# Dealing out the first loads anew, and idle matmuls that read a constant, in a local attention and gated feed-forward kernel

## The chip, the cores and the metric

The kernel runs on one core of a Trainium2 chip. The metric is device time in microseconds (us), from launch to end; three runs of the kernel before gave 213.14, 213.52 and 213.74 us.

The core has five engines that run beside each other and wait for each other through semaphores: TensorE (PE in the profile) for matrix products, VectorE (DVE), ScalarE (ACT), GpSimd (POOL) and SyncE (SP), which here issues transfers and otherwise computes nothing. Transfers (DMA) are issued by SyncE, ScalarE and GpSimd, each of which has a queue of its own.

## The reference

The input `x` has 2048 rows of 512 numbers. It is normalised by rows, and the result feeds two branches. One is an attention of 32 heads of 16 numbers in which each row sees itself and seven earlier rows, two apart. The other is a gated feed-forward layer. The two are multiplied and added to the input. Cut to what matters:

```python
xn = _layernorm(x, axis=-1)
qkv = xn @ wqkv                       # 512 -> 3 * 512, split into q, k, v of 32 heads
logits = einsum("bhsd,bhswd->bhsw", q, kg) * scale   # kg: k at s, s-2, ..., s-14
attn = softmax(where(mask, logits, -1e9))
s = einsum("bhsw,bhswd->bhsd", attn, vg) @ wo
h = gelu(xn @ w_gate) * (xn @ w_up)   # 512 -> 1792
g = silu(h @ w_down)                  # 1792 -> 512
return x + s * g
```

All inputs and the output are bf16.

## The kernel before

The 2048 rows are cut into four blocks `j` of 512 (`TQ`), and each block into four tiles of 128 rows. A block goes through these stages: normalise and transpose (`layernorm`, for tiles 0 and 1 `early_tile`), q, k and v (`qkv`, for block 0 tile by tile in `qkv_tiles`), the scores and their softmax (`scores`), the weighted sum over v (`values`), the feed-forward layer (`ffn` and `down`), and the product of the two branches with the addition of `x` and the store (`out`).

No stage is issued when it is written. Each piece of work is declared as an `Op` with a name, an engine, an estimated duration, the names that it needs (with a `~` in front: only the start of that piece), and a priority. The function `schedule` then deals these out in order of estimated time, with the priorities as tie-breakers, and the instructions are emitted in that order; so each engine has one fixed order. The figures of `PARAMS` (base priorities by stage and block, and one `nudge` for each `Op`) set the priorities.

The names that matter for this change:

- `warm` (L246) declares five pieces, `warm0` to `warm4`, of idle matmuls: their product is never read. They keep TensorE working until the first transposes. Four pieces have two matmuls of 128 x 512 columns each, the last has one of 256. Their operand is `blank`, a tile that VectorE fills with zeros (L1222) at the start of the program, ahead of the fill of `eps` (L1223).
- `preset` (L262) is an activation on ScalarE without a use of its own; it makes the table for the square root load early. In the plan it stands behind the start of `ld_wqa`.
- `early_tile` (L423) handles tiles 0 and 1 in halves of 256 columns: statistics, root, scaling, two transposes for each half (`turn`), and the copy into `xT0` (`copy`).
- `qkv_tiles` (L572) multiplies each tile by wq, wk and wv, 16 matmuls of 128 columns for each (L584). For q and k of tile 0, and q of tile 1, it is cut into two pieces of eight, such as `mm_k0_t0a` and `mm_k0_t0`: the first needs the first half of the weight (`ld_wka`) and of the transposed tile, the second needs the rest.
- `loads` (L1106) issues all loads of the inputs, in the order of the list `seq`. `ld_x0_0a` and `ld_x0_0b` are the two halves of tile 0 of `x`, `ld_wqa` and `ld_wq` the two halves (256 KB each) of wq, and so on. Before the change SyncE issues both halves of tile 1, wk, the tiles 2 and 3 as one load of 256 KB, wv and all that follows; ScalarE issues the second half of tile 0 and both halves of wq.
- `out` (L1009) ends in a store of each block: two stores of 256 KB for blocks 0 to 2, smaller ones for block 3.

In the lists below, a "full" matmul moves 512 columns, a small one 128.

Of the kernel before, what the change touches and what calls it, by code (L numbers as in the profile page):

```python
# [13 lines left out]
BF16 = mybir.dt.bfloat16  # L14
F32 = mybir.dt.float32

P = 128
# [4 lines left out]
TQ = 512  # L22
# [8 lines left out]
NC = D // P  # L31
NF = DF // P
NJ = S // TQ
TPB = TQ // P
# [26 lines left out]
    sums=(3,), psum=(0,), warm=4, slack=3.5, N=[267.5, 33.2, 480.8, 875.4], S=[194.3, -690.4, 43.8, -317.7],  # L61
    V=[-45.5, -104.1, 270.7, -195.0], Q=[-3.6, -356.0, 73.8, 32.5], F=[86.8, 80.1, 275.5, 543.3],
    Y=[-111.3, 10.6, -115.3, -110.9], O=[33.1, -472.0, -324.1, 458.9], vnorm=(), vcopy=(2,), vsum=(0,),
    crowd=1.35,
    nudge=[
# [162 lines left out]
class Kernel:  # L228
# [17 lines left out]
    def warm(self):  # L246


        def mms(i):
            if i == 0:  # L250
                self.new("warm", [P, TQ], F32, "warm_ps")
            n = TQ // 2 if i == self.par["warm"] else TQ
            for _ in range(1 if i == self.par["warm"] else 2):
                self.nc.tensor.matmul(
                    self.t["warm"][:, 0:n], lhsT=self.blank[:, 0:P], rhs=self.blank[:, 0:n], start=True, stop=True
                )

        for i in range(self.par["warm"] + 1):
            self.op(f"warm{i}", "PE", 0.95 if i < self.par["warm"] else 0.2, [f"warm{i - 1}"] if i else [], lambda i=i: mms(i),
                    take=[("F", "warm")] if i == 0 else [], use=["warm"], prio=1e6)  # L260

    def preset(self):  # L262

        self.op("preset", "ACT", 0.2, ["warm0", "~ld_wqa"], lambda: self.nc.scalar.activation(
            out=self.spare[:], in_=self.eps[:], func=AF.Sqrt), prio=-1e6, table="sqrt")
# [16 lines left out]
    def layernorm(self, j):  # L282
        base = self.when("N", j)
        for tt in range(TPB):
# [90 lines left out]
            else:  # L375
                self.op(f"stats{t}", "DVE", 0.61,
                        [f"ld_x{j if j else 2}_{j}"] + {2: ["copy1"], 3: ["~aggr2"]}.get(t, ["~rstd3"]), stats, prio=prio,
# [631 lines left out]
    def out(self, j):  # L1009
# [32 lines left out]
        if j < NJ - 1:  # L1042
# [9 lines left out]

            def store(i, j=j):
                a = j * TQ + i * 2 * P
                self.nc.sync.dma_start(
                    out=self.out2d[a : a + 2 * P, :].rearrange("(t p) d -> p t d", p=P),
                    in_=self.t[f"s16{j}"][:, 2 * i : 2 * i + 2, :],
                )
# [5 lines left out]
            for i in range(2):  # L1064
                self.op(f"store{j}_{i}", "SP", 0.35, [f"add{j}"], lambda i=i, f=store: f(i), use=[f"s16{j}"],
                        nbytes=P * TPB * D, kind="out")
# [39 lines left out]
    def loads(self, src):  # L1106
# [28 lines left out]
        def w_o():  # L1135
# [4 lines left out]
        early = [(f"ld_x{t}_0{'ab'[i]}",  # L1140
                  lambda t=t, i=i: x_tile(t, i * D // 2, (i + 1) * D // 2, "sync" if t or not i else "scalar"),
                  64 * kb if t else kb) for t in range(2) for i in range(2)]
        h = NC // 2
        wq = [("ld_wqa", lambda: w_qkv(0, 0, h, "scalar"), 256 * kb), ("ld_wq", lambda: w_qkv(0, h, NC, "scalar"), 256 * kb)]
        wk = [("ld_wka", lambda: w_qkv(1, 0, h), 256 * kb), ("ld_wk", lambda: w_qkv(1, h, NC), 256 * kb)]
# [128 lines left out]
```

## Time and profile before

| what | value |
|---|---|
| median of three runs | 213.52 us |
| lowest, highest | 213.14, 213.74 us |
| the profiled execution | 213.6 us |
| its span, first to last instruction | 211.8 us |
| TensorE busy | 206.1 us (97%) |
| VectorE busy | 187.6 us (89%) |
| ScalarE busy | 150.3 us (71%) |
| GpSimd busy | 65.5 us (31%) |
| read from memory, written | 14.12 MB, 6.31 MB |

The profile comes from one execution of its own. Its span runs from the first instruction to the last; the time of a run is longer by what lies around the span, here 1.8 us. Matmuls overlap each other, so that a duration of a single one is longer than the distance to the next: what counts for the time is the distance. Rows of the timeline merge neighbouring instructions of the same kind, and give the start, the length of the whole group, and the count. A transfer has two rows: its issue on a queue (SPq, ACTq, POOLq) and its landing, given as the time from issue to landing.

### The profile page before, as it was taken

To read this page: it belongs to the slowest core of one execution; us is meant where nothing else is said; L and a number is where in the kernel's file an instruction comes from. 1 tells how busy PE (TensorE), PEld (TensorE's weight loads), DVE (VectorE), ACT (ScalarE), POOL (GpSimd) and SP (SyncE) were. 2 spreads that over 40 slices of the span, in tenths; PEclk is the share of its full clock that TensorE was granted. 3 is DMA by queue.
4 is the path that set the end of the run, shared out by engine and by line. 5 is a ranking of instruction groups with operands and counts; after the bars stand their busy time and mean duration, and the time that the engine had idled before them with its cause. 6 is when DMAs were issued, how large, how long until landed. Compare 5 with 4: busy or idle time off the path is not lost.

```text
span 211.8 us, 3074 instructions
## 1 busy us (share of the span) xinstructions
PE 206.1 (97%) x1105; PEld 102.0 (48%) x1123; DVE 187.6 (89%) x218; ACT 150.3 (71%) x257; POOL 65.5 (31%) x107
## 2 busy tenths in 40 slices
PE   7999999999999999999999999999999999999994
PEld 2896443445444444444444444444444444444442
DVE  4788998869999998999999999999999999997024
ACT  3587957999999899766905489966614489859051
POOL 5034200002115787440459520479730011001000
PEclk9999999999999999999999999999999999999999
DMA  5999999203802888962898865358797069708903
GB/s 182 348 382 373 298 280 240 50 3 74 173 25 73 186 135 144 178 192 38 144 114 135 166 173 115 99 99 162 143 192 163 0 104 231 163 0 149 249 4 99
DMA packets 33119, 32.17 MB, mean 152 GB/s; under 512 B 17088, under 2 KB 29648, under 8 KB 33104
## 3 DMA queue, kind: packets, MB, share of 16 engines
q0 software_dynamic: 5136, 14.41, 35.8%
q1 hardware_dynamic: 27136, 16.95, 31.0%
q10 hardware_dynamic: 832, 0.62, 1.0%
q8 instruction: 9, 0.15, 0.3%
q14 instruction: 6, 0.05, 0.1%
HBM read 14.12 MB, written 6.31 MB: 96 GB/s over the span
## 4 chain that ended last, share of the span: by engine, by line
PE 94%; DMA 2%; SPq 1%; issue 1%; DVE 0%; ACT 0%
PE g_ps L900 23%; PE y_ps L960 23%; PE u_ps L900 23%; PE qkv_ps L500 15%; PE s_ps L1021 6%; PE qkv_ps L584 5%; DMA wk_sb<-in_A_wqkv_dram 2%; SPq L1110 1%; PE L_ps L716 0%; PE tr_ps L345 0%; SPq L1120 0%; DVE s L1076 0%; ACT sil L976 0%; DVE s L1082 0%
## 5 line engine op out<-in xcount | busy, mean ns | idle before, releaser
L900 PE MATMUL g_ps<-xnT,wg_sb 128*128 128x512 bf16 x221 | 54.2, 379 | 0.2
L900 PE MATMUL u_ps<-xnT,wu_sb 128*128 128x512 bf16 x217 | 52.7, 379 | 0.3
L960 PE MATMUL y_ps<-wd_sb,hT 128*128 128x512 bf16 (+2 forms) x233 | 51.4, 366 | 0.2
L916 ACT ACTIVATE gl<-g_ps 128x512 bf16<-128x512 f32 x56 | 32.6, 598 | 18.6 <-PE g_ps L900 10.8
L772 POOL DMA_DIRECT2D Ls<-prod x48 | 36.3, 844 | 29.0 <-DMA Ls<-prod 9.8
L677 DVE TENSOR_TENSOR prod<-q_sb,k_sb 128x2048 bf16<-128x2048 bf16 x32 | 38.0, 1216 | 0.7 <-ACT q_sb L515 0.7
L924 ACT ACTIVATE hT<-u_ps 128x512 bf16<-128x512 f32 x56 | 32.4, 601 | 7.2 <-PE u_ps L900 6.6
L843 DVE TENSOR_TENSOR pv<-attn,v_arr 128x4096 bf16<-128x4096 bf16 x16 | 36.1, 2283 | 0.0
L960 PEld LDWEIGHTS <-hT 128*128 128x128 bf16 x238 | 22.8, 98 | 25.9
L900 PEld LDWEIGHTS <-wu_sb 128*128 128x128 bf16 x224 | 21.8, 98 | 26.6 <-issue 0.4
L900 PEld LDWEIGHTS <-wg_sb 128*128 128x128 bf16 x224 | 21.9, 98 | 26.2
L938 DVE TENSOR_TENSOR hT<-hT,gl 128x1024 bf16<-128x1024 bf16 x28 | 18.8, 683 | 1.3 <-ACT gl L916 1.1
L691 DVE TENSOR_TENSOR prod<-prod 128x2048 bf16<-128x2048 bf16 x16 | 19.2, 1214 | 0.0
L1021 PE MATMUL s_ps<-wo_sb,oT_sb 128*128 128x512 bf16 (+2 forms) x68 | 15.1, 366 | 0.1
L976 ACT ACTIVATE sil<-y_ps 128x512 bf16<-128x512 f32 (+2 forms) x17 | 9.1, 576 | 8.6 <-PE y_ps L960 8.5
L850 DVE TENSOR_TENSOR pv<-pv 128x2048 bf16<-128x2048 bf16 x12 | 14.3, 1215 | 0.0
L649 POOL DMA_DIRECT2D v_arr<-vT_dram x16 | 10.9, 700 | 10.4 <-DMA vT_dram<-vst 10.0
L866 POOL DMA_DIRECT2D pv<-pv x4 | 3.6, 894 | 30.6 <-DVE pv L843 30.1
L515 ACT ACTIVATE q_sb<-qkv_ps 128x512 bf16<-128x512 f32 x12 | 7.1, 624 | 8.2 <-PE qkv_ps L500 8.2
L1036 ACT ACTIVATE s<-s_ps 128x512 bf16<-128x512 f32 x15 | 8.9, 602 | 5.4 <-PE s_ps L1021 5.4
L500 PE MATMUL qkv_ps<-xnT,wv_sb 128*128 128x512 bf16 x48 | 12.3, 379 | 0.0
L542 POOL DMA_DIRECT2D vT_dram<-vst x12 | 7.2, 605 | 15.7 <-ACT vst L522 15.7
(91 smaller groups left out, 231.9 us busy)
## 6 DMA issues: line engine op xcount, KB each, us to landing
Ls<-prod POOLq DMA_DIRECT2D x48, 128.0 KB, 3.7
v_arr<-vT_dram POOLq DMA_DIRECT2D x16, 142.0 KB, 4.2
vT_dram<-vst POOLq DMA_DIRECT2D x16, 128.0 KB, 3.6
pv<-pv POOLq DMA_DIRECT2D x4, 512.0 KB, 5.4
oT_dram<-o_sb SPq DMA_DIRECT2D x16, 128.0 KB, 3.4
oT_sb<-oT_dram SPq DMA_DIRECT2D x4, 512.0 KB, 4.8
wg_sb<-in_B_w_gate_dram SPq DMA_DIRECT2D x2, 896.0 KB, 10.6
wu_sb<-in_B_w_up_dram SPq DMA_DIRECT2D x2, 896.0 KB, 12.5
```

Source lines behind the costliest of these rows:

```text
L500: self.nc.tensor.matmul(ps[:], lhsT=self.w_qkv(which, dk, c), rhs=self.t[f"xT{j}"][:, dk, :], start=(dk == 0), stop=(dk == NC - 1),)
L677: self.nc.vector.tensor_tensor(out=self.t[pair][:, c % 2].rearrange("p n w t -> p w n t"), in0=q.unsqueeze(1).to_broadcast([P, W, 2, P]), ...
L691: self.nc.vector.tensor_tensor(out=pr[:, 0], in0=pr[:, 0], in1=pr[:, 1], op=ALU.add)
L772: self.nc.gpsimd.dma_start(out=self.t[f"Ls{j}"][H * tq : H * (tq + 1)], in_=self.t[f"pr{j}_{tq // 2}_0"][s::NC, 0, tq % 2], **(dict(accum_ ...
L843: self.nc.vector.tensor_tensor(out=pv[:], in0=self.t[f"at{j}"][:, 2 * i : 2 * i + 2, :].unsqueeze(2).to_broadcast([P, 2, DH, P]), in1=win, ...
L850: self.nc.vector.tensor_tensor(out=pv[:, 0], in0=pv[:, 0], in1=pv[:, 1], op=ALU.add)
L900: nc.tensor.matmul(ps[:], lhsT=w[:, dk, fc * P : (fc + 1) * P], rhs=self.t[f"xT{j}"][:, dk, :], start=(dk == 0), stop=(dk == NC - 1),)
L916: self.nc.scalar.activation(out=self.t[f"gl{j}_{pair}"][:, fc % 2, :], in_=self.t[f"ps_g{j}_{fc}"][:], func=AF.Gelu_apprx_tanh,)
L924: self.nc.scalar.activation(out=self.t[f"h{j}"][:, fc, :], in_=self.t[f"ps_u{j}_{fc}"][:], func=AF.Copy)
L938: self.nc.vector.tensor_tensor(out=h, in0=h, in1=self.t[f"gl{j}_{pair}"][:], op=ALU.mult)
L960: nc.tensor.matmul(self.t["ps_" + key][:, 0 : n1 - n0], lhsT=self.t[f"h{j}"][:, fc, tt * P : (tt + 1) * P], rhs=self.wd_sb[:, fc, n0:n1], ...
L1021: self.nc.tensor.matmul(ps[:, 0 : n1 - n0], lhsT=self.t[f"oT{j}"][:, c, tt * P : (tt + 1) * P], rhs=self.wo_sb[:, c, n0:n1], start=(c == 0 ...
```

## The change

Five things change.

1. The idle matmuls read a constant one that the program's own prologue writes into a single column, seen as a tile of 128 x 512 by strides of zero. `blank` and its fill are gone. `warm0` has three matmuls instead of two.
2. `preset` is planned behind the start of `ld_x1_0b`.
3. The first loads are dealt to the two queues in turn: SyncE has `x0` first half, `x1` first half, wq second half, wk second half; ScalarE has `x0` second half, wq first half, `x1` second half, wk first half. Tiles 2 and 3 of `x` become two loads of 128 KB on SyncE, and the statistics of each need only its own.
4. The store of block 0 is one of 512 KB instead of two of 256 KB.
5. All figures of the plan in `PARAMS` are new, among them all 858 nudges.

```diff
 PARAMS = dict(
-    sums=(3,), psum=(0,), warm=4, slack=3.5, N=[267.5, 33.2, 480.8, 875.4], S=[194.3, -690.4, 43.8, -317.7],
+    sums=(3,), psum=(0,), warm=4, slack=3.42, N=[236.5, 17.4, 498.7, 880.9], S=[216.5, -699.2, 31.7, -311.4],
...
             n = TQ // 2 if i == self.par["warm"] else TQ
-            for _ in range(1 if i == self.par["warm"] else 2):
+            ones = self.nc.const_aps.tensor(1.0, [P, TQ], BF16)
+            for _ in range(1 if i == self.par["warm"] else 2 if i else 3):
                 self.nc.tensor.matmul(
-                    self.t["warm"][:, 0:n], lhsT=self.blank[:, 0:P], rhs=self.blank[:, 0:n], start=True, stop=True
+                    self.t["warm"][:, 0:n], lhsT=ones[:, 0:P], rhs=ones[:, 0:n], start=True, stop=True
                 )
...
-            self.op(f"warm{i}", "PE", 0.95 if i < self.par["warm"] else 0.2, [f"warm{i - 1}"] if i else [], lambda i=i: mms(i),
+            self.op(f"warm{i}", "PE", 1.28 if i == 0 else 0.85 if i < self.par["warm"] else 0.2, [f"warm{i - 1}"] if i else [], lambda i=i: mms(i),
...
-        self.op("preset", "ACT", 0.2, ["warm0", "~ld_wqa"], lambda: self.nc.scalar.activation(
+        self.op("preset", "ACT", 0.2, ["~ld_x1_0b"], lambda: self.nc.scalar.activation(
...
-                        [f"ld_x{j if j else 2}_{j}"] + {2: ["copy1"], 3: ["~aggr2"]}.get(t, ["~rstd3"]), stats, prio=prio,
+                        [f"ld_x{j if j else t}_{j}"] + {2: ["copy1"], 3: ["~aggr2"]}.get(t, ["~rstd3"]), stats, prio=prio,
...
+            parts = 2 if j else 1
+            n = TPB // parts
...
-        early = [(f"ld_x{t}_0{'ab'[i]}",
-                  lambda t=t, i=i: x_tile(t, i * D // 2, (i + 1) * D // 2, "sync" if t or not i else "scalar"),
-                  64 * kb if t else kb) for t in range(2) for i in range(2)]
         h = NC // 2
-        wq = [("ld_wqa", lambda: w_qkv(0, 0, h, "scalar"), 256 * kb), ("ld_wq", lambda: w_qkv(0, h, NC, "scalar"), 256 * kb)]
-        wk = [("ld_wka", lambda: w_qkv(1, 0, h), 256 * kb), ("ld_wk", lambda: w_qkv(1, h, NC), 256 * kb)]
-        wv = [("ld_wva", lambda: w_qkv(2, 0, h), 256 * kb), ("ld_wv", lambda: w_qkv(2, h, NC), 256 * kb)]
-        x23 = [("ld_x2_0", lambda: x_block(2, 4), 256 * kb)]
+        early = [half_x(0, 0, "sync", 1), half_x(0, 1, "scalar", 1), half_x(1, 0, "sync"), half_w(0, 0, "scalar"),
+                 half_x(1, 1, "scalar"), half_w(0, 1, "sync"), half_w(1, 0, "scalar"), half_w(1, 1, "sync")]
+        early += [(f"ld_x{t}_0", lambda t=t: x_tile(t), 128 * kb) for t in (2, 3)]
+        early += [half_w(2, 0, "sync"), half_w(2, 1, "sync")]
...
-        seq = early + wq + wk + x23 + wv + [xb[1]]
+        seq = early + [xb[1]]
...
-    k.blank = cpool.tile([P, TQ], BF16, name="blank")
-    nc.vector.memset(k.blank[:].bitcast(F32), 0.0)
     nc.vector.memset(k.eps[:], EPS)
```

More of the change, by code (lines that the diff above doesn't have):

```diff
@@ L60 @@
 PARAMS = dict(
-    sums=(3,), psum=(0,), warm=4, slack=3.5, N=[267.5, 33.2, 480.8, 875.4], S=[194.3, -690.4, 43.8, -317.7],
-    V=[-45.5, -104.1, 270.7, -195.0], Q=[-3.6, -356.0, 73.8, 32.5], F=[86.8, 80.1, 275.5, 543.3],
-    Y=[-111.3, 10.6, -115.3, -110.9], O=[33.1, -472.0, -324.1, 458.9], vnorm=(), vcopy=(2,), vsum=(0,),
+    sums=(3,), psum=(0,), warm=4, slack=3.42, N=[236.5, 17.4, 498.7, 880.9], S=[216.5, -699.2, 31.7, -311.4],
+    V=[-49.3, -109.4, 272.5, -204.7], Q=[2.1, -363.3, 74.7, 33.2], F=[84.5, 80.7, 277.2, 546.4],
+    Y=[-118.9, 11.7, -116.0, -110.2], O=[36.5, -485.8, -342.3, 458.0], vnorm=(), vcopy=(2,), vsum=(0,),
     crowd=1.35,
     nudge=[
[43 rows of a table removed]
[45 rows of a table added]
     ],
@@ L1051, in add @@
                 )
+            parts = 2 if j else 1
+            n = TPB // parts
             def store(i, j=j):
-                a = j * TQ + i * 2 * P
+                a = j * TQ + i * n * P
                 self.nc.sync.dma_start(
-                    out=self.out2d[a : a + 2 * P, :].rearrange("(t p) d -> p t d", p=P),
-                    in_=self.t[f"s16{j}"][:, 2 * i : 2 * i + 2, :],
+                    out=self.out2d[a : a + n * P, :].rearrange("(t p) d -> p t d", p=P),
+                    in_=self.t[f"s16{j}"][:, n * i : n * (i + 1), :],
                 )
@@ L1063, in out @@
                     nbytes=P * TPB * D * 2, kind="acc")
-            for i in range(2):
+            for i in range(parts):
                 self.op(f"store{j}_{i}", "SP", 0.35, [f"add{j}"], lambda i=i, f=store: f(i), use=[f"s16{j}"],
-                        nbytes=P * TPB * D, kind="out")
+                        nbytes=P * n * D * 2, kind="out")
             return
@@ L1139, in loads, with half_x, half_w @@
         kb = 1024
-        early = [(f"ld_x{t}_0{'ab'[i]}",
-                  lambda t=t, i=i: x_tile(t, i * D // 2, (i + 1) * D // 2, "sync" if t or not i else "scalar"),
-                  64 * kb if t else kb) for t in range(2) for i in range(2)]
         h = NC // 2
-        wq = [("ld_wqa", lambda: w_qkv(0, 0, h, "scalar"), 256 * kb), ("ld_wq", lambda: w_qkv(0, h, NC, "scalar"), 256 * kb)]
-        wk = [("ld_wka", lambda: w_qkv(1, 0, h), 256 * kb), ("ld_wk", lambda: w_qkv(1, h, NC), 256 * kb)]
-        wv = [("ld_wva", lambda: w_qkv(2, 0, h), 256 * kb), ("ld_wv", lambda: w_qkv(2, h, NC), 256 * kb)]
-        x23 = [("ld_x2_0", lambda: x_block(2, 4), 256 * kb)]
+        def half_x(t, i, eng, size=64):
+            return (f"ld_x{t}_0{'ab'[i]}", lambda: x_tile(t, i * D // 2, (i + 1) * D // 2, eng), size * kb)
+        def half_w(w, i, eng):
+            return (f"ld_w{'qkv'[w]}" + "a" * (1 - i), lambda: w_qkv(w, i * h, (i + 1) * h, eng), 256 * kb)
+        early = [half_x(0, 0, "sync", 1), half_x(0, 1, "scalar", 1), half_x(1, 0, "sync"), half_w(0, 0, "scalar"),
+                 half_x(1, 1, "scalar"), half_w(0, 1, "sync"), half_w(1, 0, "scalar"), half_w(1, 1, "sync")]
+        early += [(f"ld_x{t}_0", lambda t=t: x_tile(t), 128 * kb) for t in (2, 3)]
+        early += [half_w(2, 0, "sync"), half_w(2, 1, "sync")]
         xb = [(f"ld_x{j}_{j}", lambda j=j: x_block(j * TPB, (j + 1) * TPB), 512 * kb) for j in range(NJ)]
-        seq = early + wq + wk + x23 + wv + [xb[1]]
+        seq = early + [xb[1]]
         seq += [("ld_wga", lambda: w_ff(w_gate, lambda: self.wg_sb, 0, half), 896 * kb)]
```

88 rows, old and new, of the table nudge are left out of this document.

## Prediction

> **What bounds the kernel now.** I read the page first, then the stages table, the chain that ended last, the timeline of the first 10 us, and the rows of the loaded tiles. The page gives the span; the stages (columns: us, then busy us and instruction count of each engine, granted clock, DMA share, GB/s) show where TensorE is idle.
>
> ```profile
> span 211.8 us, 3074 instructions
> ```
> ```profile
> 0.00:4.80 4.80, 3.54 (x9) 1.20 (x9) 2.04 (x9) 1.78 (x3) 2.88 (x20) 1.00 0.55 166
> 4.80:8.00 3.20, 2.89 (x35) 2.32 (x33) 2.00 (x9) 1.27 (x3) 0.00 (x0) 1.00 1.02 330
> 8.00:18.00 10.00, 10.00 (x177) 9.95 (x178) 8.03 (x23) 7.16 (x16) 2.28 (x3) 1.00 1.07 378
> 18.00:60.00 42.00, 41.79 (x198) 19.25 (x200) 38.36 (x51) 38.19 (x67) 5.39 (x8) 1.00 0.74 169
> 60.00:100.00 40.00, 39.79 (x183) 18.66 (x186) 39.23 (x37) 32.67 (x59) 20.49 (x30) 1.00 0.63 128
> 100.00:140.00 40.00, 39.79 (x183) 18.61 (x185) 39.51 (x38) 28.66 (x44) 18.78 (x26) 1.00 0.72 128
> 140.00:180.00 40.00, 39.79 (x183) 18.14 (x186) 39.90 (x36) 24.22 (x40) 14.80 (x19) 1.00 0.70 142
> 180.00:208.46 28.46, 28.36 (x149) 13.86 (x149) 17.78 (x22) 16.04 (x29) 0.85 (x1) 1.00 0.49 114
> ```
>
> From 8.00 to 208.46 us TensorE is busy for all but 0.21 + 0.21 + 0.21 + 0.21 + 0.10 = 0.94 us: it is the bound, and the work behind 8.00 us has a fixed length. So the end can only move by what happens before 8.00 us, by a new idle stretch behind it, or in the last 3.3 us (208.46 to 211.8), whose code the change leaves alone. The chain says the same: one piece of DMA, then TensorE to the end.
>
> ```profile
> 2.20 0.43 SPq L1120
> ...
> 2.68 5.27 DMA wk_sb<-in_A_wqkv_dram
> ...
> 8.00 3.31 PE qkv_ps L584 x56
> ```
>
> The second half of wk is issued by SyncE at 2.68 us, lands at 7.95, and TensorE goes on at 8.00. In the timeline (start, length, engine, line, operation, tiles, count, and in brackets the idle time before and its releaser) the prologue is:
>
> ```profile
> 0.38 0.11 POOL L1258 MEMSET const-bfloat16-1.0<- 128x1 bf16 x1
> ...
> 0.81 0.41 ACTq L1110 DMA_DIRECT2D x_sb<-in_A_x_dram  x1
> ...
> 0.82 1.34 SPq L1110 DMA_DIRECT2D x_sb<-in_A_x_dram  x3
> 0.93 0.27 DVE L1222 MEMSET blank<- 128x256 f32 x1 [0.93 <-PEq L1258]
> ...
> 1.25 0.47 ACTq L1120 DMA_DIRECT2D wq_sb<-in_A_wqkv_dram  x1
> ...
> 1.26 3.81 PE L254 MATMUL warm_ps<-blank 128*128 128x512 bf16 x9 [1.26 <-DVE eps L1223]
> ...
> 1.74 1.28 ACT L264 ACT_TABLE_LOAD   x1 [1.74 <-PEq L1258]
> ...
> 1.81 0.43 ACTq L1120 DMA_DIRECT2D wq_sb<-in_A_wqkv_dram  x1
> ...
> 3.04 0.20 ACT L264 ACTIVATE spare<-eps 128x1 f32<-128x1 f32 x1
> ...
> 3.98 0.29 ACT L435 ACTIVATE rstd<-mv,eps 128x1 f32<-128x1 f32 x1 [0.74 <-DVE mv L432]
> ...
> 4.51 0.60 DVE L444 TENSOR_SCALAR xn<-x_sb,mv,rstd 128x256 bf16<-128x256 bf16 x2
> ...
> 4.91 0.65 PE L452 MATMUL tr_ps<-ident,xn 128*128 128x128 bf16 x4
> 5.02 0.42 DVE L429 BATCH_NORM_STATS2 stats<-x_sb 128x6 f32<-128x256 bf16 x1
> ...
> 5.78 1.45 PE L584 MATMUL qkv_ps<-xnT,wq_sb 128*128 128x128 bf16 x16 [0.22 <-ACT xnT L459]
> ...
> 7.07 0.61 PE L584 MATMUL qkv_ps<-xnT,wk_sb 128*128 128x128 bf16 x8
> ...
> 7.99 0.48 PEld L584 LDWEIGHTS <-wk_sb 128*128 128x128 bf16 x8 [0.27 <-DMA wk_sb<-in_A_wqkv_dram]
> ...
> 8.92 1.06 PE L584 MATMUL qkv_ps<-xnT,wk_sb 128*128 128x128 bf16 x16
> ```
>
> Three losses stand here: 0.22 us until the first transposed tile is copied, 0.27 us for wk, and a slow start of the array: the first 16 matmuls of 128 columns take 1.45 us, the 16 at 8.92 take 1.06, so 0.39 us, though the granted clock reads 1.00 in every stage. Together 0.88 us, 0.4% of the time. This is nearly all that a change of the prologue can bring.
>
> **The change part by part.**
>
> *The idle matmuls.* The fill of `blank` (0.27 us of DVE) goes; the constant is written at 0.38 to 0.49. TensorE's first idle matmul waited until 1.26 for DVE's eps behind that fill; without it, it can start when the other engines do, between 0.81 (ACT queue) and 0.93 (DVE). There are now nine full ones and a half one, where there were eight and a half one:
>
> ```profile
> L254 PE MATMUL warm_ps<-blank x9: 421/634/634, 1.3 to 4.7; 128*128 128x512 bf16 x8, 128*128 128x256 bf16 x1
> ```
>
> The nine start between 1.3 and 4.7, so 0.43 apart. 9.5 x 0.43 = 4.08, and the block ends between 4.89 and 5.01, where the transposes start at 4.91 now. A loss of 0 to 0.1 us; I take 0.05. That holds if an operand with strides of zero streams like `blank`; no row has one. Bounds: at twice the pace the block ends before xn is ready and gains nothing (the first of its two operations from 4.51 is done at about 4.8), so 0; at half the pace it ends at 0.87 + 8.2 = 9.0, a loss of 4.1. The nearest row is the same instruction at 0.43, and I take that.
>
> *The table load.* It moves behind the issue of ld_x1_0b, now ScalarE's third: 0.81, 1.25, then about 1.74 to 2.2. So it runs from 2.2 to 3.5 and its activation to 3.7. The first root starts at 3.98, when DVE's mean and variance are ready: 0.25 us of cover, cost 0; beyond that each further delay reaches the transposes one for one. The next issue on ScalarE (wk's first half) is not held up: the wq issue at 1.81 ran beside the table load of 1.74.
>
> *The loads.* Landing is given per tile, as minimum, median and maximum of its loads:
>
> ```profile
> L1120 ACTq DMA_DIRECT2D wq_sb<-in_A_wqkv_dram x2: 427/446/466, 1.2 to 1.8; - x2
> ...
> DMA to landing us min/median/max: 3.1/3.4/3.8
> ```
> ```profile
> L1120 SPq DMA_DIRECT2D wk_sb<-in_A_wqkv_dram x2: 434/452/469, 2.2 to 2.7; - x2
> ...
> DMA to landing us min/median/max: 4.1/4.7/5.3
> ```
> ```profile
> L1110 SPq DMA_DIRECT2D x_sb<-in_A_x_dram x3: 393/417/433, 0.8 to 1.7; - x3
> ...
> DMA to landing us min/median/max: 2.1/2.4/3.2
> ```
>
> SyncE's order was x0a, x1a, x1b, wk first, wk second, x2 with x3, wv, wv. It becomes x0a, x1a, wq second, wk second, x2, x3, wv, wv; ScalarE's becomes x0b, wq first, x1b, wk first. SyncE issues as many loads ahead of wv as before, so wv and all that follows keep their places. What moves:
> - wk's second half goes up one place, 2.68 to 2.20: one issue of 0.47 earlier. Landing 7.95 becomes 7.5 if it takes the same 5.3 us. It is due when the four transposes of tile 1 are through, at 7.99 - 0.27 = 7.72, so the wait of 0.27 is gone: a gain of 0.27 at most, nothing more, because the matmuls before it then stand back to back.
> - wk's first half now lies behind 384 KB on ScalarE's queue, instead of behind 192 KB on SyncE's. Issue about 2.25, landing 6.3 before (2.20 + 4.1). It is due at 7.07. Cover 0.77. Bounds of its landing: 6.3 (as now) and 7.95 (as late as wk's second half is today). I take 7.1: the two halves now go side by side on queues with 640 KB each, and the midpoint of those ends is 7.1. Cost at the ends 0 and 0.88; I take 0.
> - x1's second half goes behind wq's first half, which lands at 1.25 + 3.1 = 4.35. It lands at about 4.9 now (third issue at 1.73, + 3.2) and is used at 5.02. Between 4.6 and 5.2 after: cost 0 to 0.2 on DVE, of which ScalarE's copy of tile 0 hides most, because the next root waits for that. I take 0.
> - wq's second half goes from ScalarE at 1.81 to SyncE at 1.73; it lands at 5.6 now (1.81 + 3.8) and is first read by the ninth matmul after 5.78. Cost 0.
> - x2 and x3 apart: two issues for one, in the place of the one that ScalarE took over. Their statistics run behind tile 1's copies; nothing on TensorE waits for them. 0.
>
> The Trainium skill, page "DMA: Bandwidth & Descriptors", section "Rules for kernel authors", speaks against this gain: loads spread over several issuing engines run on the same 16 DMA engines and interleave, so dealing them out saves only issue time. By it wk comes when its bytes come, and the sum would be 0 instead of -0.27; that is the first rival below. The trace leaves room for both: the DMA share is 1.02 from 4.8 to 8.0.
>
> *Stores and plan.* The first block's store becomes one of 512 KB; SyncE only waits there, 0. The new figures in PARAMS deal out the order of all engines anew. It cannot gain more than the 0.94 us of idle time behind 8.00. What it can cost is unknown; the bound is one DVE operation of the attention placed in front of something that TensorE needs: 0 to 2.28 us (row below). I take 0, since the waits of TensorE today are that small over 200 us, and keep 2.28 for the range.
>
> **Sum:** -0.27 + 0.05 = -0.22 us. The profiled execution took 213.6 us (span 211.8 and 1.8 around it), 0.1 above the median of 213.52. On the median: **213.3 us**.
>
> **The rivals.**
>
> *The same bytes, the same landing.* Ahead of wk's end lie 256 KB of x, 512 of wq and 512 of wk, 1.31 MB in either deal. By the stages 0.80 MB had come by 4.8 us and 330 GB/s follow, so these could be through at 6.35, and yet the last landed at 7.95: later loads mix in. If the two halves of wk then land together at 7.5, TensorE waits 0.43 at 7.07 for the first, does those eight matmuls (half of 16 at the later pace and a little less, 0.45) and the transposes (0.22), and reaches 8.17 instead of 8.00. With the 0.05 of the idle matmuls 213.7; at 7.95 for both 214.1. For it: the DMA is full. Against it: wq, last on its own queue, landed only 3.8 us after its issue. Chance 0.18.
>
> *The array is fast sooner.* The idle matmuls start 0.35 us earlier and there is one more. If the array runs at the later pace from the first product, 0.39 us go too, and with the wk wait 0.27, and some 0.1 of the 0.94 behind: 212.8. Against it: the weights must then be there at 6.7, not 7.07. The skill's page "TensorE: Matmul & The Clock Gate", Part 1, says that the array doubles its pace some 4 us into sustained work, at a point set by a free-running window; here it came among the 16 matmuls from 5.78 on, 4.5 to 6 us after the first idle one at 1.26, so the trace agrees roughly, and by that rule the earlier start makes this case likelier without making it sure. Chance 0.20.
>
> *A new wait behind 8 us* (the other side). DVE is busy for 39.90 of 40 us from 140 to 180, and its long operations are these:
>
> ```profile
> L843 DVE TENSOR_TENSOR pv<-attn,v_arr 128x4096 bf16<-128x4096 bf16 x16 | 36.1, 2283 | 0.0
> ```
>
> The last block's attention goes through DVE, a store and a load (issued 195.69) before TensorE can use it at 203.26; with 4.8 us to landing there are 2.8 us of cover:
>
> ```profile
> oT_sb<-oT_dram SPq DMA_DIRECT2D x4, 512.0 KB, 4.8
> ...
> 195.69 0.37 SPq L1002 DMA_DIRECT2D oT_sb<-oT_dram  x1
> ...
> 203.26 2.75 PE L1021 MATMUL s_ps<-wo_sb,oT_sb 128*128 128x512 bf16 x12
> ```
>
> If the new order makes that chain later by two such products, 4.6 us, TensorE has nothing left to fill in: 4.6 - 2.8 = 1.8 us, 215.1. It decides from 2.8 us of delay on. Chance 0.20.
>
> *The zero stride is slow.* As worked out, +4.1 us: 217.6. It costs from 0.43 us per idle matmul on, since the block ends just when xn comes. Chance 0.06.
>
> **How the numbers follow.** Forecast 0.36, and 0.18, 0.20, 0.20, 0.06. About 0.3% (0.64 us) is what a measurement of this kernel can tell from no change. Faster by more than that: the second rival and an edge of the forecast, 0.22. Within: most of the forecast and of the first rival, 0.51. Slower: the last two and the first rival's end, 0.27. The range leaves out the zero stride, the upper part of the new wait and the lowest part of the early clock: 212.6 to 215.1.
>
> **What would show it.** The first idle matmul near 0.9 us, spaced 0.43; transposes near 4.95; no wait for wk's second half and its landing near 7.5; wk's first half landing by 7.1; TensorE busy without a hole over 0.3 us behind 8 us; the last TensorE work ending near 208.2. I am wrong if TensorE waits for the first half of wk, if the transposes come later than 5.1, or if a stage behind 18 us shows TensorE idle for more than 0.5 us.

## The result, and the profile after

The changed kernel took 214.68 us (median of nine runs, 214.38 to 216.44), the kernel before 213.52 (213.14 to 214.18): slower by the ratio 1.0069, 95% interval 1.0044 to 1.0094. The forecast was 213.3, and slower had a chance of 0.27; the time lies inside the range, on the other side of the kernel before.

The profiled execution of the changed kernel took 216.44 us, 1.8 above its median; what sets it apart is told with the last experiment. The stages of its profile:

```profile
4.80:8.00 3.20, 1.80 (x22) 1.31 (x20) 1.79 (x7) 1.28 (x3) 0.00 (x0) 1.00 1.03 349
8.00:18.00 10.00, 9.66 (x144) 9.66 (x145) 6.40 (x19) 5.58 (x11) 1.53 (x2) 0.83 1.07 376
18.00:60.00 42.00, 41.79 (x233) 20.61 (x235) 38.11 (x53) 38.31 (x67) 6.69 (x10) 1.00 0.75 168
60.00:100.00 40.00, 39.79 (x183) 18.74 (x186) 38.69 (x36) 32.55 (x60) 20.01 (x29) 1.00 0.63 129
100.00:140.00 40.00, 39.79 (x183) 18.64 (x186) 39.83 (x40) 28.32 (x45) 17.03 (x24) 1.00 0.75 122
140.00:180.00 40.00, 39.84 (x185) 18.11 (x185) 39.77 (x36) 23.77 (x39) 15.62 (x20) 1.00 0.70 129
180.00:208.46 28.46, 28.30 (x132) 13.10 (x134) 18.13 (x18) 17.67 (x30) 1.72 (x2) 1.00 0.54 131
```

From 18 to 208 us TensorE is as full as before: the new plan lost nothing there. Ahead of 8 us it is busy for 1.80 of 3.20 us, where it was 2.89, and from 8 to 18 us the granted clock is 0.83. The chain of waits begins like this:

```profile
1.74 0.49 ACTq L1116
2.23 0.03 issue
2.26 0.61 ACT L267
2.88 5.42 DMA wk_sb<-in_A_wqkv_dram
8.30 0.05 issue
8.34 0.91 PE qkv_ps L587 x8
```

The transfer at the head of the chain is again a half of wk, but the other one: the first, which ScalarE issues now. It is issued at 2.88 and lands at 8.30. The timeline of the same stretch:

```profile
0.85 4.21 PE L257 MATMUL warm_ps<-const-bfloat16-1.0 128*128 128x512 bf16 x10 [0.85 <-PEq L1266]
...
2.26 1.28 ACT L267 ACT_TABLE_LOAD   x1 [2.26 <-issue]
...
2.88 0.39 ACTq L1126 DMA_DIRECT2D wk_sb<-in_A_wqkv_dram  x1
2.88 0.75 DVE L432 BATCH_NORM_STATS2 stats<-x_sb 128x6 f32<-128x256 bf16 x2 [1.94 <-DMA x_sb<-in_A_x_dram]
...
4.86 0.53 PE L455 MATMUL tr_ps<-ident,xn 128*128 128x128 bf16 x4
...
5.54 0.43 DVE L432 BATCH_NORM_STATS2 stats<-x_sb 128x6 f32<-128x256 bf16 x1 [0.50 <-DMA x_sb<-in_A_x_dram]
...
6.12 0.24 DVE L464 COPY xnT<-tr_ps 128x256 bf16<-128x256 bf16 x1
...
8.34 0.91 PE L587 MATMUL qkv_ps<-xnT,wk_sb 128*128 128x128 bf16 x8 [1.32 <-DMA wk_sb<-in_A_wqkv_dram]
```

Read three things here. The issue of wk's first half and the first statistics of tile 0 start in the same moment, 2.88: both had waited for the landing of the first half of `x0`. TensorE stands idle for 1.32 us in front of the products with wk. And VectorE waits 0.50 us for the second half of tile 1, with the copy of tile 0 behind it.

Why should the issue of wk wait for `x0`? The trace names the semaphore that each load counts up when it lands, and the one that its issue waits for. The first eight of these loads have eight semaphores, and each later one takes one of these over, in turn, and waits until the load that had it has landed. In `seq` wk's first half is the seventh load. In the compiled program, behind the table load and its activation, it has become the tenth, and takes the semaphore of the second: the half of `x0` that SyncE issues, which landed at 2.85. (The other half of `x0`, on ScalarE's queue, landed at 3.01, after wk's issue.)

### The profile page after: what moved, and what is told of

Its sections match the earlier page's. It is cut to its first block, busy times and chain, and to the rows that moved or that the text cites. A ratio compares the mean times of both kernels' runs of the same rounds, so it can differ in the third digit from the quotient of the medians.

```text
span 214.4 us, 3072 instructions
## 1 busy us (share of the span) xinstructions
PE 207.7 (97%) x1106; PEld 103.5 (48%) x1124; DVE 187.7 (88%) x217; ACT 150.6 (70%) x257; POOL 65.5 (31%) x107
## 4 chain that ended last, share of the span: by engine, by line
PE 94%; DMA 3%; ACTq 1%; issue 1%; ACT 0%; DVE 0%
PE g_ps L903 23%; PE y_ps L963 22%; PE u_ps L903 22%; PE qkv_ps L503 14%; PE s_ps L1024 6%; PE qkv_ps L587 5%; DMA wk_sb<-in_A_wqkv_dram 3%; ACTq L1116 0%; ACT L267 0%; PE L_ps L719 0%; ACTq L1126 0%; PE tr_ps L348 0%; PE tr_ps L455 0%; DVE s L1082 0%; ACT sil L979 0%
## 5 line engine op out<-in xcount | busy, mean ns | idle before, releaser
L903 PE MATMUL g_ps<-xnT,wg_sb 128*128 128x512 bf16 x220 | 53.0, 379 | 0.3
L979 ACT ACTIVATE sil<-y_ps 128x512 bf16<-128x512 f32 (+2 forms) x17 | 9.7, 586 | 9.3 <-PE y_ps L963 9.2
L503 PE MATMUL qkv_ps<-xnT,wk_sb 128*128 128x512 bf16 x47 | 12.1, 379 | 0.1
L503 PE MATMUL qkv_ps<-xnT,wq_sb 128*128 128x512 bf16 x46 | 11.7, 379 | 0.1
```

Source lines behind the costliest of these rows:

```text
L503: self.nc.tensor.matmul(ps[:], lhsT=self.w_qkv(which, dk, c), rhs=self.t[f"xT{j}"][:, dk, :], start=(dk == 0), stop=(dk == NC - 1),)
L903: nc.tensor.matmul(ps[:], lhsT=w[:, dk, fc * P : (fc + 1) * P], rhs=self.t[f"xT{j}"][:, dk, :], start=(dk == 0), stop=(dk == NC - 1),)
```

## The experiments

Theory A: the loss is TensorE's wait for wk's first half, issued late and landed late on ScalarE's queue. Theory B: two queues share the bytes, and the half lands that late wherever it is issued. Theory C: the new order of all engines costs it. Every comparison below is with the kernel before on the same chip. Except where it is said, TensorE and VectorE have the order of the changed kernel.

**One word undone.**

```diff
-                 half_x(1, 1, "scalar"), half_w(0, 1, "sync"), half_w(1, 0, "scalar"), half_w(1, 1, "sync")]
+                 half_x(1, 1, "scalar"), half_w(0, 1, "sync"), half_w(1, 0, "sync"), half_w(1, 1, "sync")]
```

> The changed kernel with one word different: SyncE, not ScalarE, issues the first half of wk (third weight load on its queue); the order of TensorE and VectorE stays as in the changed kernel. Theory A (the loss is TensorE's wait for this half, which ScalarE issued late, at 2.88 us, and which landed at 8.30): issued near 2.2 it lands by 7.2, TensorE's wait for it is under 0.3 us, time 213.4, 1.2 below the changed kernel. Theory B (the bytes of two queues are shared, the half lands near 8 wherever it is issued): wait of about 1 us stays, 214.3. Theory C (the new plan of all engines costs it, not the loads): 214.6, unchanged.

213.5 us, ratio 0.9986 (0.9961 to 1.0011). In its timeline TensorE goes from wq to wk without a wait; below it, the loads of wk, with the time from issue to landing:

```profile
6.55 0.61 PE L587 MATMUL qkv_ps<-xnT,wq_sb 128*128 128x128 bf16 x8 [0.39 <-DVE xnT L464]
7.00 0.61 PE L587 MATMUL qkv_ps<-xnT,wk_sb 128*128 128x128 bf16 x8
```
```profile
L1126 SPq DMA_DIRECT2D wk_sb<-in_A_wqkv_dram x2: 469/470/470, 2.2 to 2.7; - x2
...
DMA to landing us min/median/max: 4.3/4.4/4.5
```

The first half, issued at 2.19, landed at 6.46. One word takes back the whole loss. C falls, and so does the part of B by which the half lands that late wherever it is issued.

**Ahead of the table load.** The half stays on ScalarE, but its issue is emitted in front of `preset`.

```diff
+    wka = next(o for o in order if o.name == "ld_wka")
+    order.remove(wka)
+    order.insert([o.name for o in order].index("preset"), wka)
     for o in order:
         o.emit()
```

> The changed kernel, the first half of wk still on ScalarE's queue, but issued ahead of the table load instead of behind it. Theory A: it needs no wait for the landing of x0 then, is issued near 2.27 and lands near 7.3; TensorE's wait for it falls from 1.3 to 0.4 us or less; the table load starts near 2.7, the first root slips from 3.91 to about 4.2 and the transposes from 4.86 to about 5.15. Time 213.7. Theory B: it lands near 8 all the same, 214.4. Theory C: 214.6 or, with the later table load, 214.9.

214.07 us, ratio 1.0034 (1.0002 to 1.0066): about half of the loss is gone. Its chain and its timeline:

```profile
2.25 5.21 DMA wk_sb<-in_A_wqkv_dram
7.46 0.05 issue
```
```profile
5.32 0.54 PE L455 MATMUL tr_ps<-ident,xn 128*128 128x128 bf16 x4 [0.26 <-DVE xn L447]
6.08 1.22 PE L587 MATMUL qkv_ps<-xnT,wq_sb 128*128 128x128 bf16 x16 [0.22 <-ACT xnT L462]
7.51 0.64 PE L587 MATMUL qkv_ps<-xnT,wk_sb 128*128 128x128 bf16 x8 [0.21 <-DMA wk_sb<-in_A_wqkv_dram]
```

The issue is 0.63 us earlier, the landing 0.84, and the wait falls from 1.32 to 0.21; the transposes start 0.46 us later (4.86 to 5.32), where the expectation had 0.3. Of this the later table load explains 0.23, by which the first root is later (3.91 to 4.14); then VectorE's statistics of tile 1's first half, which landed at 4.37 where it had been 3.68, stood in front of the reciprocal. So the held issue is a good part of the loss, and not all: on SyncE's queue, issued at 2.19, the half landed 1.00 us sooner than here, issued at 2.25.

**The old deal with the new plan.** x1's second half and wk's first go back to SyncE, wq's second half to ScalarE. It was measured twice.

```diff
-                 half_x(1, 1, "scalar"), half_w(0, 1, "sync"), half_w(1, 0, "scalar"), half_w(1, 1, "sync")]
+                 half_x(1, 1, "sync"), half_w(0, 1, "scalar"), half_w(1, 0, "sync"), half_w(1, 1, "sync")]
```

> The changed kernel with the loads dealt to the two queues as before the change (SyncE: both halves of tile 1 of x, both of wk; ScalarE: both halves of wq); new plan, constant operand and split of tiles 2 and 3 stay. Theories A and B: 213.4, as the kernel before, and TensorE waits about 0.3 us or less for wk's second half. Theory C: 214.5, the loss stays with the plan.

> The kernel with the old deal and the new plan once more, beside the joined one on the same chip. If its lead over the kernel before (0.9977) is real: 0.998 again, 213.1. If it came from the scatter of the first 10 us: 1.000, 213.4.

213.12 us, ratio 0.9977 (0.9954 to 0.9999), and the second time 213.24, 0.9992 (0.9979 to 1.0004). Theory C is out: the plan costs nothing that shows here. The small lead of the first time is in part scatter of the kernel before, of whose 35 runs beside it three took 215.17 to 215.61 us at a clock of 1.0. The second interval holds 1; no version here is shown to beat the kernel before.

**The constant operand alone,** in the kernel before: ten idle matmuls on the constant, no fill.

```diff
-                    self.t["warm"][:, 0:n], lhsT=self.blank[:, 0:P], rhs=self.blank[:, 0:n], start=True, stop=True
+                    self.t["warm"][:, 0:n], lhsT=ones[:, 0:P], rhs=ones[:, 0:n], start=True, stop=True
```

> The kernel before with the constant operand alone: no fill, ten idle matmuls instead of nine; loads, table load and plan as before. Theories A, B and C alike: idle matmuls start near 0.85, 0.43 us apart, transposes at 4.85 instead of 4.91; the wait for wk's second half hides that, time 213.5, no change. The rival of the prediction (the array is fast sooner): the first 16 products take about 1.1 instead of 1.45 us, and the time is 213.1 if the wait for wk does not take it back.

213.45 us, ratio 0.9987 (0.9964 to 1.0011): nothing that can be measured. The block starts at 0.85, the transposes at 4.90 (4.91 before), and the first 16 products take 1.18 us instead of 1.45:

```profile
0.85 4.21 PE L255 MATMUL warm_ps<-const-bfloat16-1.0 128*128 128x512 bf16 x10 [0.85 <-PEq L1257]
4.90 0.65 PE L453 MATMUL tr_ps<-ident,xn 128*128 128x128 bf16 x4
5.76 1.18 PE L585 MATMUL qkv_ps<-xnT,wq_sb 128*128 128x128 bf16 x16 [0.22 <-ACT xnT L460]
7.17 0.64 PE L585 MATMUL qkv_ps<-xnT,wk_sb 128*128 128x128 bf16 x8 [0.23 <-DMA wk_sb<-in_A_wqkv_dram]
```

What they gained, TensorE gave back in the 0.23 us that it waited for wk in this execution.

**Work moved into the wait.** The changed kernel, in which TensorE does tile 1's transposes and its products with wq ahead of tile 0's products with wk (in the emitted order `mm_q0_t1` is moved directly behind `mm_q0_t1a`, and `mm_k0_t0a`, `mm_k0_t0` and their copy behind both).

> The changed kernel, loads as in it (first half of wk late on ScalarE's queue), but on TensorE the four transposes of tile 1 and its 16 products with wq stand ahead of the products of tile 0 with wk. Theory A (TensorE's wait for this half at its place in the order is the loss): 0.22 + 0.90 us of work moves into the wait, which shrinks from 1.3 us to under 0.6 (the transposes need tile 1's scaling, about 7.1 to 7.4); time 213.9. Theory B (once it has landed, the shared bytes of what follows hold TensorE up anyway): 214.5, unchanged.

214.22 us in five runs, ratio 1.0039 (1.0026 to 1.0053). It is 0.78 above the kernel before, where the changed kernel was 1.16 above: about 0.4 of the expected 0.7 came back. In its chain wk no longer stands; x1's second half does, and the work that hangs on it:

```profile
1.74 3.88 DMA x_sb<-in_A_x_dram
5.62 0.02 issue
5.64 0.44 DVE stats L432
```

**VectorE's order.** The kernel with wk's first half on SyncE and tiles 2 and 3 in one load (below), where x1's second half landed at 6.04; the copy of tile 0 (`copy0`) is emitted ahead of that half's statistics (`stats1_1`).

> The kernel of the run with wk's first half on SyncE and tiles 2 and 3 joined, with one exchange on VectorE: the copy of tile 0's second half stands ahead of the statistics of tile 1's second half, which waited for a landing at 6.04 us. Theory H (x1's second half, now behind wq on ScalarE's queue, held up that copy and so TensorE's ninth product, 0.70 us): the copy runs near 5.5, the gap of 0.70 before the second eight products falls under 0.2, time 213.2, 0.4 lower. Rival: TensorE waits the same time later, for wk or for tile 1, and the time stays at 213.6.

213.64 us, ratio 1.0011 (1.0001 to 1.0022), where the same kernel without the exchange had 213.63 us, ratio 1.0002 (0.9987 to 1.0018). TensorE's rows without and with it:

```profile
5.64 0.61 PE L587 MATMUL qkv_ps<-xnT,wq_sb 128*128 128x128 bf16 x8 [0.22 <-ACT xnT L462]
6.95 0.61 PE L587 MATMUL qkv_ps<-xnT,wq_sb 128*128 128x128 bf16 x8 [0.70 <-DVE xnT L464]
```
```profile
5.76 1.38 PE L587 MATMUL qkv_ps<-xnT,wq_sb 128*128 128x128 bf16 x16 [0.22 <-ACT xnT L462]
6.98 0.61 PE L587 MATMUL qkv_ps<-xnT,wk_sb 128*128 128x128 bf16 x8
7.43 0.53 PE L455 MATMUL tr_ps<-ident,xn 128*128 128x128 bf16 x4
7.80 0.61 PE L587 MATMUL qkv_ps<-xnT,wk_sb 128*128 128x128 bf16 x8
```

The gap of 0.70 is gone, so the mechanism is shown; the time is not shorter, as the rival said. (In this execution the half landed at 5.74, so the gap would have been smaller.) Tile 1's own transposes still hang on the late half, through its root and scaling: their group is 0.53 us long, where it was 0.41.

**Tiles 2 and 3 in one load again,** with the old deal (measured twice) and with wk's first half on SyncE. Theory D: with one load less ahead of it, wv is issued and lands earlier, and a wait of TensorE for it goes. Theory E: wv comes when its bytes come, and these are the same.

```diff
-        early += [(f"ld_x{t}_0", lambda t=t: x_tile(t), 128 * kb) for t in (2, 3)]
+        early += [(f"ld_x{t}_0", lambda t=t: x_block(2, 4) if t == 2 else None, 128 * kb) for t in (2, 3)]
```

> The kernel of the run with the old deal and the new plan, with tiles 2 and 3 of x in one load of 256 KB again. Theory D (each load waits for the landing of the one eight places ahead of it; the split pushed wv's second half onto a later one, so it was issued at 5.44 instead of 4.33 us, landed at 10.57, and TensorE waited 0.5 us): it is issued by 4.6, lands by 10.0, no wait, time 212.7. Theory E (wv comes when its bytes come, and those are the same): 213.1, unchanged.

> The joined kernel with the old deal once more. Theory D (wv's second half earlier saves TensorE's wait of 0.5 us) expects it 0.3 to 0.4 below the unjoined one; theory E expects both alike within 0.2 us; if the first comparison was no scatter, it is 0.3 above the unjoined one.

> The kernel of the run with wk's first half on SyncE, with tiles 2 and 3 of x in one load of 256 KB again (x1's second half stays on ScalarE, wq's second half on SyncE). Theory D: wv's second half is issued by 4.5 instead of 5.2, lands by 9.9 instead of 10.54, TensorE's wait of 0.4 us for it goes, time 213.1. Theory E: 213.5, unchanged.

213.48 us, ratio 1.0004 (0.9992 to 1.0016), and 213.50, 1.0003 (0.9989 to 1.0017), with the old deal; 213.63 with wk's first half on SyncE. None is 0.3 us below its unjoined kernel: the gain of theory D did not come. The wait for wv, 0.38 us, stood in the profiled execution of the unjoined kernel's first measurement (213.84 us, its longest of twelve) and not in that of the second.

**Idle matmuls inside the wait, and the changed kernel once more.** Six idle matmuls of 512 columns ahead of `mm_k0_t0a`, on the constant, into the bank that these products overwrite.

> The changed kernel with six more idle matmuls of 512 columns right ahead of the first products with wk, about 1.3 us of TensorE inside the wait; nothing else differs. Theory F (the two of nine runs near 216.4 us are those in which the array's clock was taken back after the wait): granted clock 1.00 in the stage 8 to 18 us, no run above 215.5, median 214.6 as before since the idle matmuls end before the landing at 8.30. Rival: those runs have nothing to do with the wait, and two or three of twelve are again near 216.4.

> The changed kernel itself, on the same chip as the others. Median 214.6; theory F (the array's clock is taken back after the long wait in some executions) expects about two in nine runs near 216.4 with a mean granted clock of 0.99, and none such in the kernels without the wait.

With them 214.92 us, ratio 1.0071 (1.0058 to 1.0083), five runs from 214.73 to 215.12 with a mean granted clock of 0.999 or 1.000. The idle matmuls were too long for the wait: the half landed at 8.34, and the products with it started at 8.68, which fits a median 0.3 longer than the changed kernel's.

The changed kernel again: 214.65 us, ratio 1.0088 (1.0057 to 1.0119). Of its eleven runs four took 216.17 to 217.67 us at a mean clock of 0.990 to 0.992, seven 214.48 to 214.84 at 0.998 or 1.000; in the first nine it was two. The stages of its profiled execution, one of the four:

```profile
7.00:7.50 0.50, 0.14 (x3) 0.00 (x0) 0.50 (x2) 0.32 (x1) 0.00 (x0) 1.00 1.09 385
7.50:8.00 0.50, 0.00 (x0) 0.00 (x0) 0.00 (x0) 0.28 (x1) 0.00 (x0) 1.00 1.10 365
8.00:8.50 0.50, 0.31 (x4) 0.32 (x5) 0.00 (x0) 0.00 (x0) 0.00 (x0) 0.51 1.13 346
...
9.00:10.00 1.00, 1.00 (x13) 1.00 (x11) 0.52 (x3) 0.00 (x0) 0.00 (x0) 0.50 1.11 358
10.00:11.00 1.00, 1.00 (x12) 1.00 (x11) 0.97 (x3) 0.45 (x1) 0.00 (x0) 0.50 1.06 371
11.00:12.00 1.00, 1.00 (x17) 1.00 (x15) 0.98 (x4) 0.33 (x2) 0.00 (x0) 0.79 1.05 382
```

Behind the wait the granted clock is 0.50 for some 3.4 us, which costs 1.7 us: about the distance between the two groups of runs. In the traces this low stretch goes from 8.01 to 11.43 us here and from 8.55 to 11.96 in the first profile of the changed kernel. In every trace the record of the clock changes only at times that lie 3.41 us or a multiple of it apart; where these times lie differs from execution to execution. TensorE's busy time in the stretch of 3.41 us just ahead of the loss, here and in the first profile:

```profile
4.60:8.01 3.41, 2.06 (x22) 1.25 (x20) 2.11 (x8) 1.27 (x3) 0.00 (x0) 1.00 1.07 370
```
```profile
5.14:8.55 3.41, 1.67 (x24) 1.30 (x23) 1.55 (x6) 1.28 (x3) 0.00 (x0) 1.00 1.03 354
```

The kernel with the idle matmuls in the wait kept its clock. Its stretch with the most idle time was this:

```profile
4.32:7.73 3.41, 2.39 (x25) 1.55 (x24) 2.15 (x9) 0.84 (x3) 0.00 (x0) 1.00 1.06 349
```

No other stretch ahead of 200 us, in any of the fourteen traces, was busy for less than that once the full clock had begun. At the end of the program, where TensorE runs out of work, every trace loses the clock as well, always at the end of a stretch that was busy for 1.35 us or less; near the end, stretches with 1.62 and 2.00 us kept it. So it was lost in thinly filled stretches of 3.41 us alone, with no sharp limit between 1.62 and 2.06 us of busy time.

That the long wait brings the loss about, in those executions in which it falls into one stretch, is therefore likely. It is not proven: two profiled executions lost the clock there, and the five runs with idle matmuls that had no loss, where six of twenty had it, could be chance (0.17 without any effect). The kernel with the half ahead of the table load had two such runs of twelve. The kernel with tile 1 first had none in five, the six kernels with no long wait for that half none in 92 runs, and the kernel before none in the 90 runs beside them: there the mean clock was 0.997 or more.

## Why the prediction was wrong, point by point

- **The bound** was read rightly: only the first 8 us could move the end, and at full clock only they did. TensorE's idle time behind 18 us is that of before.
- **The idle matmuls** were right: 0.43 apart with strides of zero, transposes at 4.80 to 4.95 in most kernels with the table load in place. The rival of a slow zero stride is out.
- **The failed step is "wk's first half", with "cover 0.77" and "I take 0".** It failed in two places. The issue was put at 2.25, since an issue on ScalarE had run beside the table load before; that reason holds, but the load had also changed its place among all the loads, and so waited for the landing of `x0`: 2.88. In four executions of the changed load order its issue and the first statistics of `x0` start together, at 2.85, 2.88, 2.94 and 2.99. Then it was given a landing at 7.1, the midpoint between 6.3 and 7.95, with the bytes ahead of it counted on its own queue; it landed at 8.30, later than the later end. TensorE's wait was 1.32 us (1.04 in the second profile), where even the later end had 0.88, and the median rose by 1.16 us. TensorE waiting for this half is one of the signs of being wrong that the prediction named.
- **Why it landed so late** can be read from the traces together. Count the bytes of the loads in the order of their issue on both queues. The half of a weight that completes the first 1024 KB landed between 6.15 and 7.13 us in thirteen of the fourteen profiled executions, on whichever queue; the one that completes 1280 KB landed between 7.21 and 8.30. wk's first half completes 1024 KB in the kernel before (6.27) and on SyncE's queue (6.46). Ahead of the table load, it is issued 0.05 us behind wk's second half and completes 1280 KB: 7.46, with the second half at 7.26. In the changed kernel `x2`, issued at 2.71, is ahead of it too, and it completes 1408 KB: 8.30, and 8.14 to 8.34 in the other three traces of this load order. So the held issue and the new deal both put bytes ahead of it, and its own queue is the wrong place to count them.
- **What was said of SyncE's loads,** that wv and all that follows keep their places, was wrong too: wv's first half went from 3.70 to 4.44. SyncE has as many loads ahead of it as before, but with `x2` and `x3` apart it is the eleventh load of all and not the tenth, and so waits for the landing of wq's first half (4.42) where it had waited for `x0`'s (2.93). It cost nothing that could be measured.
- **"x1's second half: I take 0"** was wrong in its reason. It landed at about 5.5 in the changed kernel (4.9 before) and at 5.6 to 6.0 in others of that deal. ScalarE's copy does not hide it, because VectorE has tile 0's second copy in its order behind that half's statistics. In the changed kernel the longer wait for wk covers most of it.
- **The gain of 0.27:** wk's second half did land earlier, at 6.70 (7.5 was forecast), but now the first half came behind it. And the wait of 0.27 was one draw. The landing of wk's second half, issued at 2.67 or 2.68 as in the trace of before, was 7.95 there, 7.51 with the old deal (its second run) and 8.30 with the old deal and one load for tiles 2 and 3 (its second run). A wait that is read in a single execution of so crowded a stretch is no term of that size.
- **The rivals.** "The same bytes, the same landing" had the place right, TensorE waiting for the first half, and a time up to 214.1 (its own terms give 214.2). Its reason fits the traces too, if the bytes are counted in the order of issue; it counted both halves of wk and left out `x2`. The Trainium skill's rule that spreading loads over issuing engines doesn't help ("DMA: Bandwidth & Descriptors", "Rules for kernel authors") agrees with the four deals without the late half, all within 0.4% of the kernel before. (With wk's gain at nothing the sum is +0.05, the term of the idle matmuls, and not 0 as the prediction has it there.) "The array is fast sooner" was seen in single executions (16 products in 1.07 or 1.18 us), and no median shows it. With the same ten idle matmuls from 0.85, the record of the clock shows the full clock from 3.63 us on in one execution and only from 6.49 in another: when it comes is a matter of the execution. "A new wait behind 8 us" did not come.

What stays open: whether the order of issue alone sets these landings. The runs compared differ in more than that, and no run has ScalarE issue wk's first half ahead of SyncE's issue of the second. Nor is it known why a half issued at the same time in the same order lands so differently: wk's first half at 6.27 us in the kernel before and at 7.13 with the constant operand alone.

## What to carry to other kernels

A load moved to another queue takes a new place in three orders: that of the queue, with all its instructions; that of the completion semaphores, where it may have to wait for an older load to land; and that of all loads by their time of issue, which here told best when its bytes came. Work out all three before its landing is estimated. Give a moved load the later end of its bounds as its landing, and let it be one that the first waiting engine can do other work in front of. And a stretch in which many loads land together should be read from several executions before a wait in it is counted as a gain.

## What the runs showed of the hardware

An idle stretch of 1.0 to 1.3 us of TensorE, after 4 us of busy time, was followed in some executions by 3.41 us at a granted clock of 0.50. The Trainium skill ("TensorE: Matmul & The Clock Gate", Part 1) has the clock fall after an idle window of about 3.4 us; here no single idle stretch was that long. The measurement decides: in the two profiled executions that lost the clock there, TensorE was busy for 1.67 and 2.06 us of the 3.41 us ahead of the loss, and a stretch with 2.39 us kept it. Busy time alone does not decide: near the end of the program one with 1.62 us kept it too. Six of twenty executions of the changed kernel show the loss in their mean clock.

Loads landed nearly in the order of their issue on both queues, and not queue by queue: the half of a weight that completes the first 1024 KB landed between 6.15 and 7.13 us in thirteen of fourteen traces, on whichever queue.
